# The bonus term of a recurrent attention: from token-major vector work to one d-major product, small matmuls and a seeded PSUM bank

## The chip, the cores and the metric

The kernel runs on one core of one Trainium2 chip, as one program of 961.6 us in the profiled execution. The metric is the device time of the whole program in microseconds, the median of the runs. The engines are named as the profile names them: PE is the matmul engine and PEld its weight loads, DVE the vector engine, ACT the scalar engine, POOL GpSimd, SP the engine that issues most DMAs.

## The reference

The reference chains three parts: a recurrent attention, a capacity-limited mixture of experts on its output, and a second feed-forward network for all tokens. The change touches only the first part:

```python
def _attn_ref(r, k, v, w, u):
    B, H, S, D = r.shape                     # 4, 8, 768, 48
    state = np.zeros((B, H, D, D))
    for t in range(S):
        cur = einsum('bhd,bhe->bhde', u[None] * kt, vt)
        y[:, :, t] = einsum('bhd,bhde->bhe', rt, state + cur)
        state = wt[:, :, :, None] * state + einsum('bhd,bhe->bhde', kt, vt)
```

The term with `cur` is the bonus. Written out, it is for each token and head the number c = sum over d of r·u·k, times the row v of that token: y = r·state + c·v. The 3072 x 384 result y is the input of the routing (logits = y times an 8-column gate) and of the experts (8 experts, 384 tokens each), whose output goes through a network of width 2048.

## The kernel before, in words

The attention is cut into 24 chunks (`NU`) of 128 tokens, six for each of the four batch rows, in the order chunk 0 of all rows, chunk 1 of all rows, and so on. Within a chunk the recurrence is a product of matrices. Two scans along time on DVE (`scans`, L203 and L210) give running products of the decays, Q and Ap. With them, k and r are scaled (`khrh`, L217 on KH, L218 on RH; on POOL except in the first chunks). They are d-major: the 48 features of two heads lie on 112 partitions, the 128 tokens of four head pairs in the free dimension. The steps of a chunk are then:

- `scores` (L265): eight matmuls, KH times RH for each head, into two PSUM tiles `sc`; `scores_ev` (L272): DVE multiplies them with a triangular mask into P.
- `tr` (L253): KH transposed into the bank `pk`; `vp` (L246): v times the gate's weights, also into `pk`. So each head's v carries, behind its 48 columns, 8 columns that make the logits (`vx`, 56 columns a head). ACT copies both out (`vp_ev` L249, `tr_ev` L257).
- `ymm` (L281, L283): state part and score part of y, into the bank `py` (128 x 8 x 56); `umm` (L291): the chunk's addition to the state, into `pu`; `sadd` (L301): DVE adds it to the state `Sb`; `decay` (L306): ACT scales the state.
- the bonus: `rku` (L230, L232) on POOL multiplies token-major r, u and k; `cred` (L237) on DVE sums over the 48 features to c; `cvf` (L242) on POOL makes c times v with its 8 gate columns; `xev` (L313, L320, L316) on DVE adds it to `py`, once for the logits and once for the output `xt`, and reduces the logits over the heads. `xst` stores `xt` to DRAM for the gather of the experts.

The order on each engine is that of the Python code; there is no scheduler that moves it. A loop over n writes, for each n, the PE work of scores(n), tr(n), vp(n), ymm(n-1), umm(n-1), then the DVE work of xev(n-2), scans(n+2), sadd(n-2), scores_ev(n), then ACT's and POOL's. A piece of DVE's other work is threaded in: from n = 8 on parts of a conversion of the last network's weights (`bit`, L850 to L856), from n = 6 on comparisons for the routing (L599), and every fourth n the best expert of four chunks (`top`, L591 to L594). `warm` (L331) issues products of a constant tile into an unused bank before scores(n): 13 ahead of the first chunk, and as `WARMS` says 6, 4 and 2 at n = 1, 3 and 4.

PSUM has few buffers: three for `sc` (two are used per chunk), two for `py`, one each for `pk` and `pu`. So scores(n) needs scores_ev(n-1) for its second tile, and umm(n-1) needs sadd(n-2).

After the attention, from 240 us on, come the routing of the first expert and then eight slots of expert work, which the change does not touch.

Of the kernel before, what the change touches and what calls it, by code (L numbers as in the profile page):

```python
# [9 lines left out]
F32 = mybir.dt.float32  # L10
# [16 lines left out]
E = 8  # L27
# [36 lines left out]
LATE = 4  # L64
# [3 lines left out]
WARMS = {1: 6, 2: 0, 3: 4, 4: 2}  # L68
# [4 lines left out]
class Kernel:  # L73
# [11 lines left out]
    # ------------------------------------------------------------- constants  # L85
# [59 lines left out]
    # ------------------------------------------------- attention, chunk by chunk  # L145
    def attention(self):
        tc, nc, t = self.tc, self.nc, self.t
        with ExitStack() as ctx:
# [9 lines left out]
            ub = A.tile([128, DM], F32, name="ub")  # L158
# [28 lines left out]
            def load2(n):  # L187
                c, b = divmod(n, B)
                d = T[n]
                if n == 0:  # L190
                    nc.sync.dma_start(self.ident, t["cst"][:, 128:256])
                    nc.sync.dma_start(WG, t["wg"])
                nc.sync.dma_start(d["vT"], t["vT"][b, :, c * CH:(c + 1) * CH].rearrange("(a p) t -> p a t", p=128))
                nc.sync.dma_start(d["rkv"], t["rkv"][n])
                if n == 0:
                    nc.sync.dma_start(ub, t["cst"][:, 256:640])
# [29 lines left out]
            def rku(n):  # L226
                d = T[n]
                rk = d["rkv"]
                ku = wk.tile([128, DM], F32, tag="ku", name=f"ku{n}", bufs=2)
                nc.gpsimd.tensor_tensor(ku, rk[:, DM:2 * DM], ub, op=ALU.mult)  # L230
                d["rku"] = wk.tile([128, H, D], F32, tag="rku", name=f"rku{n}", bufs=2)
                nc.gpsimd.tensor_tensor(d["rku"].rearrange("p a b -> p (a b)"), rk[:, 0:DM], ku, op=ALU.mult)  # L232

            def cred(n):
                d = T[n]
                d["cc"] = wk.tile([128, H], F32, tag="cc", name=f"cc{n}")
                nc.vector.tensor_reduce(d["cc"], d["rku"], axis=AX.X, op=ALU.add)  # L237

            def cvf(n):
                d = T[n]  # L240
                d["cv"] = wk.tile([128, H, XW], F32, tag="cv", name=f"cv{n}", bufs=2)
                nc.gpsimd.tensor_tensor(d["cv"], d["vx"], d["cc"].unsqueeze(2).to_broadcast([128, H, XW]), op=ALU.mult)  # L242
# [32 lines left out]
            def ymm(n):  # L275
                d = T[n]
                c, b = divmod(n, B)
                py = d["py"] = ps_y.tile([128, H, XW], F32, tag="py", name=f"py{n}")
                for p in range(NP):
                    if c > 0:  # L280
                        nc.tensor.matmul(py[:, 2 * p:2 * p + 2].rearrange("p a b -> p (a b)"), d["rh"][:R, p], Sb[b][:, p], start=True, stop=False)  # L281
# [3 lines left out]
            def umm(n):  # L285
                d = T[n]
                d["pv"] = ps_u.tile([128, NP, XW], F32, tag="pu", name=f"pu{n}")
# [19 lines left out]

            def xev(n):
                d = T[n]
                d["xt"] = wk.tile([128, H, D], F32, tag="xt", name=f"xt{n}")  # L310
                py = d["py"]
                lg = wk.tile([128, H, E], F32, tag="lg", name=f"lg{n}")
                nc.vector.tensor_tensor(lg, py[:, :, D:], d["cv"][:, :, D:], op=ALU.add)  # L313
                if n < NU - 1:
                    xev2(n)
                nc.vector.tensor_reduce(self.L[:, n], lg.rearrange("p h e -> p e h"), axis=AX.X, op=ALU.add)  # L316

            def xev2(n):
                d = T[n]
                nc.vector.tensor_tensor(d["xt"], d["py"][:, :, :D], d["cv"][:, :, :D], op=ALU.add)  # L320
# [49 lines left out]
            rku(0)  # L370
# [22 lines left out]
            for n in range(NU + 2):  # L393
# [14 lines left out]
                # tensor engine  # L408
                warm(WARMS.get(n, 0))
                if ok(n):  # L410
                    scores(n)
                if ok(n):
                    pk = ps_k.tile([128, 512], F32, tag="pk", name=f"pk{n}")
# [4 lines left out]
                if n == NU - 1:  # L418
                    pb = ps_u.tile([1, 1], F32, tag="pu", name="pb")
                    nc.tensor.matmul(pb, bs[:, 1:2], one, start=True, stop=True)  # L420
                if ok(n - 1):
                    ymm(n - 1)
                if ok(n - 1) and n - 1 < NU - B:
                    umm(n - 1)
                # vector engine
# [3 lines left out]
                if ok(n) and n >= LATE:  # L429
                    cred(n)  # L430
                if n in (2, 3):
                    xev(n - 2)
                    sadd(n - 2)
# [7 lines left out]
                if ok(n - 2) and n > 3:  # L441
                    xev(n - 2)
                next(sg, None)
                if ok(n - 2) and n - 2 < NU - B and n > 3:
                    sadd(n - 2)
                next(sg, None)
# [5 lines left out]
                if n < LATE:  # L452
                    cred(n)
# [9 lines left out]
                if n == NU + 1:  # L463
# [3 lines left out]
                    xev2(NU - 1)  # L467
                # scalar engine
                if ok(n + 1) and n + 1 >= B:
                    decay(n + 1)  # L470
                if ok(n - 2):
                    xst(n - 2)
                if ok(n):
                    vp_ev(n, pk)
                if n < NU - B:
                    tr_ev(n, pk)
# [7 lines left out]
                # gpsimd  # L484
# [3 lines left out]
                if ok(n - 1):  # L488
                    cvf(n - 1)
# [8 lines left out]
                if ok(n + 1):  # L498
                    rku(n + 1)
# [13 lines left out]
    # ------------------ the recurrence step by step, for decays outside [WLO, WHI]  # L513
# [66 lines left out]
    # -------------------------------------------- best expert of each token  # L580
# [33 lines left out]
    def search(self, ph, mk, es, ve):  # L614
        """the expert that fills, and its tokens above the threshold and at it"""
# [47 lines left out]
            # which of them suffice, and the largest  # L663
# [49 lines left out]
    # ------------------ one expert's fill: threshold, tokens, list of token ids.  # L713
    # Yields after each group of vector work and after each group of tensor work.
    def fill(self, ph):
# [4 lines left out]
        if ph == E - 1:  # L720
            # one expert has room: its tokens up to here, and just enough room for all that are left
# [20 lines left out]
        # places in the list, from 1: those above first, then those at it  # L742
# [8 lines left out]
        # place 16 a + b: the ids where b fits, one where a fits, and their product  # L751
# [27 lines left out]
        # place 128 g + j: the ids spread over the partitions j  # L779
# [16 lines left out]
        # what is left for the next one  # L796
# [26 lines left out]
    # ------------------------------------------------------- weights in two parts  # L823
# [19 lines left out]
    def io_bits(self, i):  # L843
        """moe2 weights come as 64-bit floats: their float32 value from the bits"""
# [27 lines left out]
    def io_stages(self):  # L872
        """two pieces at a time, a part of the vector work per step; the other engines follow later"""
# [45 lines left out]
    # ------------------------------------------------------------------ one expert  # L919
# [24 lines left out]
    def slot(self, p, dve, pe, tick):  # L944
# [4 lines left out]
        def product(ps, w):  # L949
            """w: three pairs of parts"""  # L950
# [94 lines left out]
    def rows(self, i):  # L1045
        """the result for the i-th list of tokens: no token is in two lists, so no list waits for another"""
# [122 lines left out]
    def left(self, p):  # L1169
        """the routing after slot p's list and up to the next one"""  # L1170
# [20 lines left out]
def layout(r, k, v, w, u, moe_w_gate, moe_w1, moe_w2, moe2_w_in, moe2_w_out):  # L1191
# [19 lines left out]
    rkv = np.concatenate([token(r).reshape(NU, CH, DM), token(k).reshape(NU, CH, DM), ve.reshape(NU, CH, H * XW)], 2)  # L1211
# [6 lines left out]
    ub = np.broadcast_to(u.reshape(1, DM), (128, DM))  # L1218
# [5 lines left out]
    cst = np.concatenate([mask, np.eye(128, dtype=f), ub], 1)  # L1224
# [21 lines left out]
    a = dict(kr=kr, wp=wp, rkv=rkv, vT=vT, wg=wg, wgp=wgp, uc=uc, cst=cst, kst=kst, w12=w12, wio=wio)  # L1246
# [15 lines left out]
```

## Time and profile before

| | us |
|---|---|
| median of 3 runs | 962.47 (962.35 to 963.18) |
| span of the profiled execution | 961.6 |
| attention, first scores to last y | 8.5 to 240.1 |
| PE busy / DVE busy / ACT busy / POOL busy | 888.7 / 606.9 / 377.6 / 499.8 |

The profile lists one execution. Its span runs from the first to the last instruction, and the timed runs lie about 0.9 us above it. A busy engine is not always a useful one: a DVE instruction's time holds the time for which it was held up while it ran, and a matmul's time depends on the clock that the throttle granted to PE at that moment. That clock has a line of its own on the page, in tenths of the full one.

### The profile page before, as it was taken

How to read it: one execution, taken by the hardware profiler on the slowest of the kernel's cores; microseconds unless marked ns; L12 is line 12 of the kernel's file. 1: busy time of each engine (PE TensorE's matmuls, PEld its weight loads, DVE VectorE, ACT ScalarE, POOL GpSimd, SP SyncE). 2: the span in 40 equal slices, each digit the busy share in tenths (PEclk: the TensorE clock that was granted, in tenths of full speed). 3: DMA queues.
4: the chain of work that ended last, by engine and by line, in shares of the span. 5: the costliest groups of instructions: out<-in, count | busy, mean ns of one | idle time of the engine just before them, and what ended most of it. 6: DMA issues, size and time to landing. Idle time of an engine off the chain costs nothing.

```text
span 961.6 us, 15248 instructions
## 1 busy us (share of the span) xinstructions
PE 888.7 (92%) x5658; PEld 839.9 (87%) x5661; DVE 606.9 (63%) x1333; ACT 377.6 (39%) x865; POOL 499.8 (52%) x441
## 2 busy tenths in 40 slices
PE   7899989999257989999999999999999999999997
PEld 5788978999246979899989999998999999999996
DVE  9999999996789897654466265446635542232211
ACT  3244334330134444344434534443353444334332
POOL 6888756763567356424622732562373365256232
PEclk8675575555567999999999999999999999999999
DMA  9877776620454003102301310220130032023000
GB/s 289 255 223 214 222 212 202 213 82 26 161 189 148 1 0 124 59 1 78 104 1 50 91 42 1 91 91 1 51 107 25 1 107 75 1 75 107 1 1 25
DMA packets 40356, 90.06 MB, mean 94 GB/s; under 512 B 4304, under 2 KB 17104, under 8 KB 40272
## 3 DMA queue, kind: packets, MB, share of 16 engines
q1 hardware_dynamic: 32016, 70.12, 23.7%
q0 software_dynamic: 3072, 9.44, 3.0%
q10 hardware_dynamic: 5184, 9.44, 2.8%
q8 instruction: 46, 0.75, 0.3%
q14 instruction: 38, 0.31, 0.1%
HBM read 79.54 MB, written 9.44 MB: 93 GB/s over the span
## 4 chain that ended last, share of the span: by engine, by line
PE 64%; DVE 28%; issue 3%; DMA 1%; ACT 1%; POOL 1%; POOLq 0%; SPq 0%; ACTq 0%; DVEq 0%
PE pg L953 18%; PE ph L953 8%; PE py L1002 6%; PE py L1004 6%; PE py L1003 6%; PE py L283 3%; DVE cm L647 3%; PE pa L979 3%; PE pa L977 3%; PE pa L978 3%; DVE Ap L210 3%; PE py L281 2%; DVE q L856 2%; DVE Q L203 2%; PE sc L265 2%
## 5 line engine op out<-in xcount | busy, mean ns | idle before, releaser
L994 POOL TENSOR_TENSOR gl<-r,gh 128x384 fp32r<-128x384 f32 x126 | 133.4, 1062 | 268.2 <-ACT gh L993 268.0
L990 DVE SCALAR_TENSOR_TENSOR r<-r,pg 128x384 f32<-128x384 f32 x128 | 70.7, 552 | 158.3 <-ACT r L989 156.4
L953 PE MATMUL pg<-xh,io 128*128 128x384 f32 x768 | 160.8, 344 | 0.0
L906 POOL TENSOR_TENSOR wl<-we,wh 128x768 fp32r<-128x768 f32 x60 | 112.6, 1878 | 59.6 <-ACT wh L905 39.8
L953 PEld LDWEIGHTS pg<-xh,io 128*128 128x128 f32 x768 | 132.2, 188 | 2.6 <-ACT xh L1021 1.6
L1004 PE MATMUL py<-io,gl 128*128 128x384 f32 x384 | 130.4, 340 | 1.7 <-POOL gl L994 1.7
L1002 PE MATMUL py<-io,gh 128*128 128x384 f32 x384 | 131.8, 343 | 0.0
L1003 PE MATMUL py<-io,gh 128*128 128x384 f32 x384 | 129.5, 337 | 0.0
L989 ACT ACTIVATE r<-pg,three 128x384 f32<-128x384 f32 x128 | 74.3, 580 | 118.0 <-PE pg L953 108.3
L993 ACT ACTIVATE gh<-r 128x384 fp32r<-128x384 f32 x128 | 67.2, 525 | 108.6 <-DVE r L990 108.6
L953 PE MATMUL pg<-xl,io 128*128 128x384 f32 x384 | 87.5, 336 | 0.0
L283 PE MATMUL py<-rkv,P 128*128 128x56 f32 x384 | 82.0, 366 | 0.0
L283 PEld LDWEIGHTS py<-rkv,P 128*128 128x128 f32 x384 | 81.5, 298 | 0.0
L971 DVE SCALAR_TENSOR_TENSOR hl<-ph,hh 128x384 fp32r<-128x384 f32 x62 | 34.4, 555 | 68.8 <-ACT hh L970 68.7
L1004 PEld LDWEIGHTS py<-io,gl 128*128 128x128 f32 x384 | 72.4, 189 | 2.7 <-POOL gl L994 2.4
L1002 PEld LDWEIGHTS py<-io,gh 128*128 128x128 f32 x384 | 72.5, 189 | 0.2
L1003 PEld LDWEIGHTS py<-io,gh 128*128 128x128 f32 x384 | 72.6, 189 | 0.0
L905 ACT ACTIVATE wh<-we 128x768 fp32r<-128x768 f32 x64 | 53.6, 838 | 40.6 <-PE pa L979 28.8
L953 PE MATMUL ph<-xh,wh 128*128 128x384 f32 x192 | 68.7, 358 | 0.1
L953 PEld LDWEIGHTS pg<-xl,io 128*128 128x128 f32 x384 | 68.6, 188 | 0.0
L979 PE MATMUL pa<-hl,wh 128*128 128x384 f32 x192 | 65.8, 343 | 0.8 <-POOL hl L968 0.7
L977 PE MATMUL pa<-hh,wh 128*128 128x384 f32 x192 | 66.3, 345 | 0.0
(202 smaller groups left out, 1820.8 us busy)
## 6 DMA issues: line engine op xcount, KB each, us to landing
we<-in_w SPq DMA_DIRECT2D x64, 384.0 KB, 3.1
rkv<-in_rkv SPq DMA_DIRECT2D x24, 608.0 KB, 6.3
kr<-in_kr SPq DMA_DIRECT2D x24, 448.0 KB, 6.4
raw<-in_wio SPq DMA_DIRECT2D x20, 384.0 KB, 6.3
w<-in_wp SPq DMA_DIRECT2D x24, 226.2 KB, 4.4
vT<-in_vT SPq DMA_DIRECT2D x24, 192.0 KB, 4.8
xd<-xt ACTq DMA_DIRECT2D x24, 192.0 KB, 2.9
raw<-in_wio ACTq DMA_DIRECT2D x12, 384.0 KB, 4.4
```

The source lines that it names most:

```text
L283: nc.tensor.matmul(py[:, h], d["P"][h % 2][:, p], d["vx"][:, h], start=(c == 0), stop=(c == 0 or h % 2 == 1))
L906: eng.tensor_tensor(lo, raw, hi, op=ALU.subtract)
L953: nc.tensor.matmul(ps, w[a][part], x[:, a], start=(n == 0), stop=(n == 8))
L977: nc.tensor.matmul(pa[d], wh[:, c], hh, start=(f == 0), stop=False)
L979: nc.tensor.matmul(pa[d], wh[:, c], hl, start=False, stop=(f == NFT - 1))
L989: nc.scalar.activation(g, ph, AF.Relu, bias=self.three)
L990: nc.vector.scalar_tensor_tensor(g, g, 6.0, ph, op0=ALU.min, op1=ALU.mult)
L993: nc.scalar.activation(gh, g, AF.Copy)
L994: (nc.vector if last and f >= NGT - 2 else nc.gpsimd).tensor_tensor(gl, g, gh, op=ALU.subtract)
L1002: nc.tensor.matmul(py[q], gh[:, c], w, start=(f == 0), stop=False)
L1003: nc.tensor.matmul(py[q], gh[:, c], v, start=False, stop=False)
L1004: nc.tensor.matmul(py[q], gl[:, c], w, start=False, stop=(f == NGT - 1))
```

## The change

The bonus is computed another way. `bonus` forms r times k d-major, from the k and r tiles that are loaded anyway, in one DVE multiplication of 112 x 512. `cc` gets c from it with four small matmuls against a constant `UB` that holds u (two columns per pair of heads), into free columns of the bank of `pu`; ACT copies the 8 columns out (`cc_ev`). `seed` writes c times v, with its gate columns, into the bank of `py`: eight ACT instructions of 128 x 56, one per head, with c as the scale. The matmuls of `ymm` then accumulate onto it (start=False everywhere; one product into each of the two `py` buffers at the start of the program sets the state of the bank). So `py` is the finished y: DVE only reduces the logits from it (`logits`), and ACT copies the output (`xev`). POOL loses three multiplications per chunk, DVE three instructions per chunk. The token-major r and k are no longer loaded: 224 KB a chunk for v in place of 608 KB.

The products of the constant tile are now issued in `scores`, into the chunk's own first `sc` tile: 6 for n = 1, none for n = 0 and 2, and 4 for every n from 3 on. Comments were dropped too; they are left out below.

```diff
-LATE = 4
-WARMS = {1: 6, 2: 0, 3: 4, 4: 2}
+WARMS = 0, 6, 0, 4
...
-                d["rkv"] = io.tile([128, 2 * DM + H * XW], F32, tag="rkv", name=f"rkv{n}", bufs=6)
-                d["vx"] = d["rkv"][:, 2 * DM:].rearrange("p (h e) -> p h e", e=XW)
+                d["v"] = io.tile([128, H * XW], F32, tag="v", name=f"v{n}", bufs=6)
+                d["vx"] = d["v"].rearrange("p (h e) -> p h e", e=XW)
...
-            def rku(n):
...
-                nc.gpsimd.tensor_tensor(ku, rk[:, DM:2 * DM], ub, op=ALU.mult)
...
-                nc.gpsimd.tensor_tensor(d["rku"].rearrange("p a b -> p (a b)"), rk[:, 0:DM], ku, op=ALU.mult)
-            def cred(n):
...
-                nc.vector.tensor_reduce(d["cc"], d["rku"], axis=AX.X, op=ALU.add)
-            def cvf(n):
...
-                nc.gpsimd.tensor_tensor(d["cv"], d["vx"], d["cc"].unsqueeze(2).to_broadcast([128, H, XW]), op=ALU.mult)
+            def bonus(n):
+                d["rk"] = wk.tile([R, NP, CH], F32, tag="rk", name=f"rk{n}")
+                nc.vector.tensor_tensor(d["rk"], d["kr"][:, 0], d["kr"][:, 1], op=ALU.mult)
+            def cc(n, pu):
+                d["pc"] = pu[:, 448:448 + H]
+                for p in range(NP):
+                    nc.tensor.matmul(pu[:, 448 + 2 * p:450 + 2 * p], d["rk"][:, p], UB[:, 2 * p:2 * p + 2], start=True, stop=True)
+            def cc_ev(n):
+                nc.scalar.activation(d["cc"], d["pc"], AF.Copy)
+            def seed(n):
+                py = d["py"] = ps_y.tile([128, H, XW], F32, tag="py", name=f"py{n}")
+                for h in range(H):
+                    nc.scalar.activation(py[:, h], d["vx"][:, h], AF.Copy, scale=d["cc"][:, h:h + 1])
...
             def scores(n):
+                for _ in range(WARMS[min(n, len(WARMS) - 1)]):
+                    nc.tensor.matmul(d["sc"][0].rearrange("p a b -> p (a b)"), wz[:, :128], wz, start=True, stop=True)
...
             def ymm(n):
-                py = d["py"] = ps_y.tile([128, H, XW], F32, tag="py", name=f"py{n}")
+                py = d["py"]
...
-                        nc.tensor.matmul(py[:, h], d["P"][h % 2][:, p], d["vx"][:, h], start=(c == 0), stop=(c == 0 or h % 2 == 1))
+                        nc.tensor.matmul(py[:, h], d["P"][h % 2][:, p], d["vx"][:, h], start=False, stop=True, skip_group_check=True)
...
+            def logits(n):
+                nc.vector.tensor_reduce(self.L[:, n], T[n]["py"][:, :, D:].rearrange("p h e -> p e h"), axis=AX.X, op=ALU.add)
             def xev(n):
-                nc.vector.tensor_tensor(lg, py[:, :, D:], d["cv"][:, :, D:], op=ALU.add)
...
-                nc.vector.tensor_reduce(self.L[:, n], lg.rearrange("p h e -> p e h"), axis=AX.X, op=ALU.add)
-                nc.vector.tensor_tensor(d["xt"], d["py"][:, :, :D], d["cv"][:, :, :D], op=ALU.add)
+                nc.scalar.activation(d["xt"], d["py"][:, :, :D], AF.Copy)
...
-            rku(0)
+            for i in range(2):
+                first = ps_y.tile([128, H, XW], F32, tag="py", name=f"first{i}")
+                nc.tensor.matmul(first.rearrange("p a b -> p (a b)"), wz[:, :128], wz[:, :H * XW], start=True, stop=True)
+            bonus(0)
+            bonus(1)
+            pu = ps_u.tile([128, 512], F32, tag="pu", name="pu_")
+            cc(0, pu)
```

PE's order around one chunk, in the kernel before. `pu15` is umm of chunk 15, `cnt8` a sum for the routing, `sc17` the scores of chunk 17, `pk17` its transposes and its gate product:

```order
L291 MATMUL pu15_1757<-rkv15_1122,kt15_1699 48x56 x8
L609 LDWEIGHTS cm8_9_1716
L609 MATMUL cnt8_910<-oh_89,cm8_9_1716 128x8
...
L265 MATMUL sc17_0_1825<-RH2_133,KH2_130 128x128
L265 MATMUL sc17_1_1826<-RH2_133,KH2_130 128x128
...
L253 MATMUL pk17_1835<-ident_72,KH2_130 128x112 x4
L246 MATMUL pk17_1835<-WG_119,vT17_1322 128x64 x3
```

The same place in the changed kernel, after umm of chunk 11; `rk13` is the product r times k of chunk 13, `wz` the constant tile:

```order
L298 MATMUL pu12_1484<-v11_784,kt11_1412 48x56 x8
L234 MATMUL pu12_1484<-UB_118,rk13_1395 128x2 x4
...
L267 LDWEIGHTS wz_136
L267 MATMUL sc13_0_1557<-wz_136 128x512
...
L271 MATMUL sc13_0_1557<-RH1_132,KH1_129 128x128
L271 MATMUL sc13_1_1558<-RH1_132,KH1_129 128x128
...
L257 MATMUL pk13_1571<-ident_72,KH1_129 128x112 x4
L250 MATMUL pk13_1571<-WG_119,vT13_998 128x64 x3
L287 MATMUL py12_1526<-Sb0_123,RH0_131 128x112
```

Four matmuls for c of the next chunk stand behind umm, and four products of the constant tile ahead of the scores; the y of a chunk stands a whole step behind its gate product, as before.

DVE's order in the step n = 13 of the kernel before. `cc13` is cred, Q15 and Ap15 are the scans of chunk 15, `q3` is weight conversion, `lg11`, `xt11` and L belong to xev:

```order
L237 TENSOR_REDUCE cc13_1468<-rku13_1413 128x8
L203 SCALAR_TENSOR_TENSOR Q15_1470<-w15_1119,b1_120 112x517
L206 TENSOR_SCALAR G15_1473<-Q15_1470 112x4
L852 TENSOR_SCALAR q3_1301<-q3_1301 128x384
L313 TENSOR_TENSOR lg11_1477<-py11_1347,cv11_1407 128x64
L320 TENSOR_TENSOR xt11_1476<-py11_1347,cv11_1407 128x384
L316 TENSOR_REDUCE L_87<-lg11_1477 128x8
L208 RECIPROCAL b2_1_122<-G15_1473 112x4
L301 TENSOR_TENSOR Sb3_126<-Sb3_126,pu11_1360 48x4x56 x2
L210 SCALAR_TENSOR_TENSOR Ap15_1471<-w15_1119,b2_1_122 112x517
L272 TENSOR_TENSOR P13_0_1485<-sc13_0_1428,mask_117 128x512
L272 TENSOR_TENSOR P13_1_1487<-sc13_1_1429,mask_117 128x512
```

The same step of the changed kernel; `rk15` is the new multiplication:

```order
L316 TENSOR_REDUCE L_87<-py11_1414 128x8
L201 SCALAR_TENSOR_TENSOR Q15_1607<-w15_1218,b1_120 112x517
L204 TENSOR_SCALAR G15_1610<-Q15_1607 112x4
L858 TENSOR_SCALAR q3_1426<-q3_1426 128x384
L206 RECIPROCAL b2_1_122<-G15_1610 112x4
L308 TENSOR_TENSOR Sb3_126<-Sb3_126,pu12_1484 48x4x56 x2
L228 TENSOR_TENSOR rk15_1616<-kr15_1219 112x512
L208 SCALAR_TENSOR_TENSOR Ap15_1608<-w15_1218,b2_1_122 112x517
L278 TENSOR_TENSOR P13_0_1619<-sc13_0_1557,mask_117 128x512
L278 TENSOR_TENSOR P13_1_1621<-sc13_1_1558,mask_117 128x512
```

The three instructions on `cc`, `lg` and `xt` are gone, the logits' reduction has moved to the head of the step, and one multiplication has come in ahead of the second scan.

PE's first chunk in the kernel before:

```order
L331 MATMUL pw_137<-wz_136 128x512
L265 MATMUL sc0_0_249<-RH0_131,KH0_128 128x128
...
L253 MATMUL pk0_259<-ident_72,KH0_128 128x112 x4
L246 MATMUL pk0_259<-WG_119,vT0_155 128x64 x3
L331 LDWEIGHTS wz_136
```

And in the changed kernel, where `first0` and `first1` are the two products into the `py` buffers:

```order
L373 MATMUL first0_235<-wz_136 128x448
...
L373 MATMUL first1_237<-wz_136 128x448
L234 MATMUL pu__243<-UB_118,rk0_239 128x2 x4
L271 MATMUL sc0_0_258<-RH0_131,KH0_128 128x128
...
L257 MATMUL pk0_268<-ident_72,KH0_128 128x112 x4
L250 MATMUL pk0_268<-WG_119,vT0_155 128x64 x3
L234 MATMUL pu0_290<-UB_118,rk1_241 128x2 x4
```

The first scores now stand behind the four matmuls that read `rk0`, which DVE makes after RH of chunks 0 and 1.

## Rows read from the trace of the kernel before

**Rows 1.** The page, part 2: PE's granted clock in 40 equal slices

```profile
PEclk8675575555567999999999999999999999999999
```

**Rows 2.** Stretches: us, busy us of each engine (instructions), granted clock, DMA

```profile
42.70:76.10 33.40, 29.05 (x262) 27.04 (x261) 32.82 (x56) 13.84 (x42) 27.81 (x31) 0.80 0.79 241
76.10:147.40 71.30, 65.85 (x478) 62.43 (x478) 70.25 (x120) 26.54 (x80) 50.74 (x50) 0.58 0.70 208
147.40:199.00 51.60, 51.60 (x340) 49.28 (x340) 50.91 (x85) 18.74 (x56) 35.60 (x30) 0.50 0.68 215
199.00:240.20 41.20, 41.20 (x248) 39.88 (x246) 32.19 (x71) 7.96 (x24) 19.18 (x17) 0.50 0.07 25
```

**Rows 3.** Timeline of PE, one chunk at half clock: start, us, instruction

```profile
157.68 2.08 PE L265 MATMUL sc<-RH,KH 64*128 64x128 f32 x16
...
160.49 1.41 PE L246 MATMUL pk<-WG,vT 128*128 128x64 f32 x6
161.69 0.71 PE L281 MATMUL py<-Sb,RH 112*128 112x112 f32 x2
...
168.00 2.08 PE L265 MATMUL sc<-RH,KH 64*128 64x128 f32 x16
```

**Rows 4.** Timeline of PE, one chunk at full clock

```profile
134.06 0.60 PE L291 MATMUL pu<-rkv,kt 128*48 128x56 f32 x16
...
134.73 1.54 PE L265 MATMUL sc<-RH,KH 64*128 64x128 f32 x16
136.20 0.60 PE L253 MATMUL pk<-ident,KH 112*128 112x112 f32 x4
136.64 0.79 PE L246 MATMUL pk<-WG,vT 128*128 128x64 f32 x6
137.27 0.43 PE L281 MATMUL py<-Sb,RH 112*128 112x112 f32 x2
...
137.93 0.43 PE L281 MATMUL py<-Sb,RH 112*128 112x112 f32 x2
```

**Rows 5.** Timeline of PE: constant products, scores, and idle time with its cause

```profile
12.21 1.46 PE L331 MATMUL pw<-wz 128*128 128x512 bf16 x6
13.59 1.41 PE L265 MATMUL sc<-RH,KH 64*128 64x128 f32 x16
...
144.40 0.99 PE L291 MATMUL pu<-rkv,kt 128*48 128x56 f32 x16 [4.29 <-DVE Sb L301]
```

**Rows 6.** Groups of DVE, 76.1 to 199 us: instructions, busy us, mean ns

```profile
L599 DVE TENSOR_SCALAR cm<-kst,m 128x256 bf16<-128x256 f32 x12 | 12.0, 1001 | 0.0
...
L320 DVE TENSOR_TENSOR xt<-py,cv 128x384 f32<-128x384 f32 x12 | 6.5, 545 | 0.0
...
L237 DVE TENSOR_REDUCE cc<-rku 128x8 f32<-128x384 f32 x12 | 6.5, 540 | 0.0
```

**Rows 7.** Timeline: the comparison of L599 while POOL is idle

```profile
236.09 0.35 DVE L599 TENSOR_SCALAR cm<-kst,m 128x256 bf16<-128x256 f32 x1
```

**Rows 8.** Groups of DVE, 147 to 240 us: the one RH in it

```profile
L218 DVE TENSOR_TENSOR RH<-kr,Ap 112x512 f32<-112x512 f32 x1 | 0.7, 677 | 0.0
```

**Rows 9.** Groups of POOL, 76.1 to 199 us

```profile
L217 POOL TENSOR_TENSOR KH<-kr,Q 112x512 f32<-112x512 f32 x13 | 26.3, 2025 | 0.0
...
L232 POOL TENSOR_TENSOR rku<-rkv,ku 128x384 f32<-128x384 f32 x12 | 15.2, 1264 | 0.9
L230 POOL TENSOR_TENSOR ku<-rkv,ub 128x384 f32<-128x384 f32 x12 | 14.0, 1164 | 0.0
L242 POOL TENSOR_TENSOR cv<-rkv,cc 128x448 f32<-128x448 f32 x12 | 11.2, 935 | 28.9 <-ACT rkv L249 28.9
```

**Rows 10.** Groups of ACT, 76.1 to 199 us: the decay of the state

```profile
L306 ACT ACTIVATE Sb<-Sb,G 112x112 f32<-112x112 f32 x51 | 15.4, 372 | 0.0
```

**Rows 11.** Timeline of the start: DVE's RH of chunk 1 and first P

```profile
11.94 1.25 DVE L218 TENSOR_TENSOR RH<-kr,Ap 112x512 f32<-112x512 f32 x1
...
13.11 1.27 DVE L272 TENSOR_TENSOR P<-sc,mask 128x512 f32<-128x512 f32 x2
```

More of the change, by code (lines that the diff above doesn't have):

```diff
@@ L157, in attention @@
             mask = A.tile([128, 128], F32, name="mask")
-            ub = A.tile([128, DM], F32, name="ub")
+            UB = A.tile([R, H], F32, name="UB")
             WG = A.tile([128, 3, 64], F32, name="WG")
@@ L224, in check @@
                 nc.scalar.activation(jk, wv, AF.Relu, bias=cb[:, 1:2], scale=1.0, accum_out=acc[:, 2 * n + 1:2 * n + 2])
[L226 removed]
+            def bonus(n):
                 d = T[n]
[L228 to L234 removed]
+                d["rk"] = wk.tile([R, NP, CH], F32, tag="rk", name=f"rk{n}")
+                nc.vector.tensor_tensor(d["rk"], d["kr"][:, 0], d["kr"][:, 1], op=ALU.mult)
+            def cc(n, pu):
+                d = T[n]
+                d["pc"] = pu[:, 448:448 + H]
+                for p in range(NP):
+                    nc.tensor.matmul(pu[:, 448 + 2 * p:450 + 2 * p], d["rk"][:, p], UB[:, 2 * p:2 * p + 2], start=True, stop=True)
+            def cc_ev(n):
                 d = T[n]
                 d["cc"] = wk.tile([128, H], F32, tag="cc", name=f"cc{n}")
[L237 to L239 removed]
+                nc.scalar.activation(d["cc"], d["pc"], AF.Copy)
+            def seed(n):
                 d = T[n]
[L241 to L242 removed]
+                py = d["py"] = ps_y.tile([128, H, XW], F32, tag="py", name=f"py{n}")
+                for h in range(H):
+                    nc.scalar.activation(py[:, h], d["vx"][:, h], AF.Copy, scale=d["cc"][:, h:h + 1])
             def vp(n, pk):
@@ L277, in ymm, with umm @@
                 c, b = divmod(n, B)
-                py = d["py"] = ps_y.tile([128, H, XW], F32, tag="py", name=f"py{n}")
+                py = d["py"]
                 for p in range(NP):
                     if c > 0:
-                        nc.tensor.matmul(py[:, 2 * p:2 * p + 2].rearrange("p a b -> p (a b)"), d["rh"][:R, p], Sb[b][:, p], start=True, stop=False)
+                        nc.tensor.matmul(py[:, 2 * p:2 * p + 2].rearrange("p a b -> p (a b)"), d["rh"][:R, p], Sb[b][:, p],
+                                         start=False, stop=False, skip_group_check=True)
                     for h in (2 * p, 2 * p + 1):
-                        nc.tensor.matmul(py[:, h], d["P"][h % 2][:, p], d["vx"][:, h], start=(c == 0), stop=(c == 0 or h % 2 == 1))
-            def umm(n):
+                        nc.tensor.matmul(py[:, h], d["P"][h % 2][:, p], d["vx"][:, h], start=False, stop=True, skip_group_check=True)
+            def umm(n, pu):
                 d = T[n]
-                d["pv"] = ps_u.tile([128, NP, XW], F32, tag="pu", name=f"pu{n}")
+                d["pv"] = pu[:, 0:NP * XW].rearrange("p (a b) -> p a b", b=XW)
                 for p in range(NP):
@@ L420, in attention @@
                     nc.tensor.matmul(pb, bs[:, 1:2], one, start=True, stop=True)
+                if ok(n):
+                    cc_ev(n)
+                    if n == 0:
+                        vp_ev(0, pk)
+                        tr_ev(0, pk)
+                        seed(0)
                 if ok(n - 1):
                     ymm(n - 1)
-                if ok(n - 1) and n - 1 < NU - B:
-                    umm(n - 1)
+                if ok(n + 1):
+                    pu = ps_u.tile([128, 512], F32, tag="pu", name=f"pu{n}")
+                    if ok(n - 1) and n - 1 < NU - B:
+                        umm(n - 1, pu)
+                    cc(n + 1, pu)
                 bits["room"] = 0 if n < B0 else BITS[n % 4]
@@ L428, in attention @@
                     scores_ev(n)
[L429 to L433, printed above, removed]
+                if ok(n - 2):
+                    logits(n - 2)
                 sg = scans(n + 2) if ok(n + 2) else iter(())
@@ L440, in attention @@
                     flag = nc.values_load(self.bad[0:1, 0:1], min_val=0, max_val=128)
-                if ok(n - 2) and n > 3:
-                    xev(n - 2)
                 next(sg, None)
-                if ok(n - 2) and n - 2 < NU - B and n > 3:
+                if ok(n - 2) and n - 2 < NU - B:
                     sadd(n - 2)
+                if ok(n + 2):
+                    bonus(n + 2)
                 next(sg, None)
@@ L451, in attention @@
                     scores_ev(n)
-                if n < LATE:
-                    cred(n)
                 bit()
@@ L466, in attention @@
                     counted = []
-                    xev2(NU - 1)
+                if ok(n - 2):
+                    xev(n - 2)
+                    xst(n - 2)
                 if ok(n + 1) and n + 1 >= B:
                     decay(n + 1)
-                if ok(n - 2):
-                    xst(n - 2)
-                if ok(n):
+                if ok(n) and n:
                     vp_ev(n, pk)
-                if n < NU - B:
-                    tr_ev(n, pk)
+                    if n < NU - B:
+                        tr_ev(n, pk)
+                    seed(n)
                 if ok(n + 2):
@@ L1217, in layout @@
     wgp = np.ascontiguousarray(moe_w_gate.reshape(3, 128, E).transpose(1, 0, 2))
-    ub = np.broadcast_to(u.reshape(1, DM), (128, DM))
+    ub = np.zeros((R, H), f)
+    ub[0:D, 0::2] = u[0::2].T
+    ub[64:64 + D, 1::2] = u[1::2].T
     uc = np.zeros((R, NP), f)
```

23 lines of the change are left out of this document (5 added, 18 removed).

## The prediction

> **What bounds the kernel now.** I read the table of stretches first, then PE's timeline in two of them, then the groups of DVE and POOL. The page's line of the granted clock [rows 1] shows where to look: from the seventh slice to the fourteenth, inside the attention, PE mostly runs at half clock (1.2 of 2.4 GHz); behind the attention it is at the full one, and the change does nothing there. In the stretches [rows 2] the reader is to see that from 147.4 to 240.2 us PE is busy all the time at a granted 0.50, and that before, from 76.1 on, PE (65.85 of 71.30) and DVE (70.25) are both nearly full. So there is no slack on one engine to hide work of the other. The step of a chunk at half clock, from scores to scores, is 168.00 - 157.68 = 10.32 us [rows 3]. From chunk 8 (76.1) to chunk 20 (199.0) twelve steps take 122.9 us, 10.24 each: PE's length at half clock. At full clock the same work is: addition to the state and the routing's sum 134.73 - 134.06 = 0.67, scores 1.47, transposes 0.44, gate product 0.63, and four groups of y of 0.66 each, 2.64 [rows 4]; in all 5.85 us. DVE would then be the longer one. Before chunk 8 the steps are shorter: four take 33.4 us, 8.35 each, at a mean clock of 0.80 [rows 2], and DVE is the full engine (32.82).
>
> **PE, added.** Four matmuls for c, in fp32 as the gate product is, whose three cost 161.69 - 160.49 = 1.20 us at half clock [rows 3] and 0.63 at full [rows 4]. Their moving side is 2 columns in place of 64, but each has its own weight load of 128 columns as there, so I take the gate product's price: 1.60 at half, 0.84 at full clock. From below it could be a third of that, if the narrow side counted. Four products of the constant tile: six took 13.59 - 12.21 = 1.38 us at full clock [rows 5], so four are 0.92, and about 1.84 at half. The step of PE becomes 5.85 + 0.84 + 0.92 = 7.6 us at full clock and 10.32 + 1.60 + 1.84 = 13.8 at half. Nothing is taken off PE. So the change stands or falls with the clock: the step equals the old 10.24 when (10.24 - 7.6) / (13.8 - 7.6) = 43% of its work runs at half clock.
>
> **PE's clock.** The rows on this: the six products at 12.2 us ran at full clock with the scores behind them (1.41 us instead of 2.08) [rows 5, 3]. Of the steps without such products, from chunk 8 on, most stayed at half clock although PE did not pause (51.60 of 51.60 us) [rows 2]; one rose by itself to 0.67 a group of y [rows 4], and fell back around a wait of 4.29 us for the state's addition on DVE [rows 5]. So a long run of wide products lifts the clock, narrow ones behind weight loads don't, and an idle PE loses it. In the changed kernel each step from chunk 3 on has the wide products and the scores in one piece. I expect a rise in each step at the latest behind the scores, and a fall wherever DVE makes PE wait. If products and scores are paid at half clock and the rest at full, the step is 1.84 + 2.01 + (7.6 - 0.92 - 1.47) = 9.1 us.
>
> The Trainium skill (TensorE: Matmul & The Clock Gate, Why this matters for your kernels) says that matmul throughput is had by keeping TensorE busy without a break. By that rule the stretch at 147 us would already be at full clock and the dummy products would be nothing but cost; the rows, 100% busy at 0.50, are against it.
>
> **DVE.** Off: cred 0.540 and xt 0.545 us [rows 6], and the smaller addition of the logits; the reduction of the logits stays. On: one multiplication 112 x 512 of two SBUF tiles, the size of RH: 0.68 us where POOL left DVE alone [rows 8], 1.25 next to POOL [rows 11]. By itself that is between -0.6 and +0.1 a step. More comes from POOL: the comparison of L599 takes 0.35 us when POOL is idle [rows 7] and 1.00 on the mean of the busy stretch [rows 6], where it runs beside ku and rku. POOL loses ku, rku and cv, 1.16 + 1.26 + 0.94 = 3.4 us a step [rows 9]. That is 0.65 for this instruction, and I take as much again for the scan, the conversion and the little ones that stand in the same shadow; bounds 0 and 2. A DVE step near 10.2 so becomes about 8.6 (9.4 to 7.6).
>
> The Trainium skill (SBUF — State Buffer, Who interferes with whom) has a rule that speaks against the new multiplication: a DVE instruction with two SBUF inputs and a POOL instruction that reads SBUF exclude each other for their whole length, while those removed here read one SBUF input at most. By it `rk` can wait for a KH (2.03 us on the mean [rows 9]) and the step would keep up to 10.6; RH's 1.25 against 0.68 agrees that such a pair holds the other up, but not for a whole KH.
>
> **ACT, POOL, DMA.** ACT gets eight instructions of 128 x 56 with a scale from memory; the decay, 112 wide, takes 0.37 [rows 10], so at most 3.0 a step, plus the output, 0.55 as on DVE, and a copy of 8 columns. It was busy 18.74 of 51.60 us [rows 2], 3.7 a step; it will be busy about 7.5. That hides, since y of a chunk stands a whole step behind its gate product: between them PE has the y, the state's addition and the scores before, at least 5 us, against 0.5 + 3.0 on ACT. Without that cover PE would wait up to 3 us a step. The waits behind a seed on ACT (the check of a later chunk) are early for everyone. DMA moves a quarter less, and was 0.70 busy [rows 2]; at nothing.
>
> **The start.** The matmuls for c of chunk 0 stand ahead of the first scores, and wait for a multiplication that DVE makes behind RH of chunk 1 (ends at 13.19, [rows 11]): first P at about 13.2 + 0.7 + 1.6 + 2.0 = 17.5 us, against 13.11. That is 4.4 us late on an engine that is the full one here. About 3.4 of it should come back by chunk 4, where POOL no longer holds up the scans. +1, bounds -2 and +4.
>
> **The sum**, against the profiled execution (961.6 us; the median is 0.9 above it):
>
> - to 42.7 us: +1
> - four steps to 76.1: 8.35 to 8.0 (PE's clock keeps them from less): -1.4
> - twelve steps to 199: 10.24 to 9.2, between PE's mixed step 9.1 and DVE's 8.6 with their hand-over: -12.5
> - 199 to 240.2, no weight conversion, no state: three steps of 9.65, 8.6 and 8.6 to about 7.5, -4.4; the last scores and two y, 14 us at half clock, to 10.5: -3.5. Together -8
> - after 240.2: 0
>
> -20.9: 940.7 in the span, 942 with what lies around it. With each step from 7.9 to 10.0 the sum runs from 926 to 953.
>
> **Rivals.**
>
> *Full clock and a free DVE.* PE has so little idle time that the clock holds, and POOL's absence is worth 2 us a step. Steps of 8.0: 12 x 2.24 = -27, -3 before, -9 after, +1 at the start: 925. For it: 7.6 fits under DVE's step. Against: then PE waits, and in the trace waits cost the clock.
>
> *The gain is spent.* The rise comes late in each step, or the new multiplication takes up what POOL gave back. The twelve steps stay at 10.2, the end gains 3, the start costs 1: 960.
>
> *Slower: the added PE work is paid at half clock.* The place is the step from chunk 4 on. PE gets 2.4 bound steps more; above 43% of the work at half clock the twelve steps are longer than before. At 60%: 7.6 + 0.6 x 6.2 = 11.3; 12 x 1.1 = +13 and 4 x 2.5 = +10 before (c of the first four chunks has no state part, so it is less than 2.95), +1: 986. All at half clock would be 1030. For it: the trace has 54 us in which full PE work left the clock at 0.50. Against: the rows with constant products.
>
> **How the numbers follow.** Forecast 942: 0.58. Full clock, 925: 0.16. Spent, 960: 0.10, half of it below the bound. Slower, 986: 0.16. A measurement of this kernel tells 0.2%, 1.9 us, from no change. Faster: 0.58 + 0.16 + 0.05 = 0.79; same 0.04; slower 0.17. The likeliest case's own range is 931 to 953. The range that holds 8 in 10 reaches from 922 to 964: it leaves out the slower case but its edge, and the fastest end.
>
> **What would show it.** Right: a granted clock of 0.7 to 0.9 from 76 to 240 us in place of 0.50 to 0.58, scores of 1.4 us behind constant products, steps near 9, L599 well below 1.0 us, ACT near 7.5 us a step without PE waiting for a seed, the first P near 17.5. Wrong: a clock still at 0.5 with PE full and steps above 10.3 (the slower rival), PE idle ahead of y with ACT as its releaser (the cover of the seed gone), or `rk` of 2 us and more beside KH.

## The result, and the profile after

The changed kernel takes 917.92 us (914.75 to 920.66, 4 runs) against 962.41 (962.16 to 963.18, 4 runs): a ratio of 0.954, with a 95% interval of 0.951 to 0.957. The forecast was 942, with a range of 922 to 964; the gain, 44.5 us in place of 20.5, is more than twice the forecast one. Runs over 1.5% above the fastest of their kernel count as slow and stay out of the ratios: below, these are three of the four without products and one of `start`.

The first thing to read is the page's line of the granted clock, which answers to [rows 1]. The long run of fives to sevens there is gone; the dip that is left begins in the ninth slice (183 to 206 us), behind the last y (197 us), in the routing:

```profile
PEclk8899999985879999999999999999999999999998
```

Then the stretches, cut at the same chunks as [rows 2]: scores of chunk 4, 8 and 20, and the last y. The columns are us, busy us of PE, PEld, DVE, ACT and POOL (instructions), granted clock, DMA share, GB/s:

```profile
0.00:43.95 43.95, 34.23 (x266) 27.18 (x269) 37.31 (x62) 24.47 (x74) 13.77 (x22) 0.84 0.92 257
43.95:75.00 31.05, 30.47 (x304) 25.98 (x307) 26.00 (x49) 27.22 (x88) 11.59 (x22) 0.92 0.72 222
75.00:166.80 91.80, 89.51 (x950) 79.04 (x961) 89.05 (x170) 78.16 (x248) 41.62 (x37) 0.99 0.64 194
166.80:197.00 30.20, 28.66 (x270) 25.47 (x273) 25.71 (x62) 22.89 (x73) 8.56 (x7) 1.00 0.09 34
```

| stretch | forecast | measured |
|---|---|---|
| to chunk 4 (before 42.70) | +1 | +1.25 |
| four steps to chunk 8 (33.40) | -1.4 | -2.35 |
| twelve steps to chunk 20 (122.90) | -12.5 | -31.1 |
| to the last y (41.20) | -8 | -11.0 |
| behind it | 0 | -0.7 |
| sum | -20.9 | -43.9 |

So 18.6 of the 23 us that the forecast missed lie in the twelve steps: 7.65 us each, forecast 9.2. PE's timeline shows one of them (start, us, instruction). PE hardly pauses, each piece is at full clock, and from scores to scores it is 112.72 - 105.34 = 7.38 us:

```profile
105.34 1.16 PE L271 MATMUL sc<-RH,KH 64*128 64x128 f32 x16
106.43 0.60 PE L257 MATMUL pk<-ident,KH 112*128 112x112 f32 x4
106.87 0.79 PE L250 MATMUL pk<-WG,vT 128*128 128x64 f32 x6
107.50 0.43 PE L287 MATMUL py<-Sb,RH 112*128 112x112 f32 x2
...
110.27 0.60 PE L298 MATMUL pu<-v,kt 128*48 128x56 f32 x16
110.80 1.05 PE L234 MATMUL pu<-UB,rk 112*128 112x2 f32 x8
111.72 0.19 PE L615 MATMUL cnt<-oh,cm 128*128 128x8 bf16 x2
111.98 0.81 PE L267 MATMUL sc<-wz 128*128 128x512 bf16 x3
112.72 1.16 PE L271 MATMUL sc<-RH,KH 64*128 64x128 f32 x16
```

The matmuls for c take 111.72 - 110.80 = 0.92; the routing's sum and the four products (the profile lists three) 1.00. DVE's busy time is 89.05 us for twelve chunks, 7.42 each, against 10.10 before (70.25 and 50.91 us, [rows 2]). Its groups in that stretch (instructions, busy us, mean ns, idle before):

```profile
L208 DVE TENSOR_TENSOR_SCAN Ap<-w,b 112x517 f32<-112x517 f32 x12 | 18.7, 1554 | 0.0
L201 DVE TENSOR_TENSOR_SCAN Q<-w,b 112x517 f32<-112x517 f32 x11 | 14.7, 1340 | 0.0
L278 DVE TENSOR_TENSOR P<-sc,mask 128x512 f32<-128x512 f32 x22 | 14.2, 685 | 0.3
L228 DVE TENSOR_TENSOR rk<-kr 112x512 f32<-112x512 f32 x12 | 9.1, 756 | 0.4
L605 DVE TENSOR_SCALAR cm<-kst,m 128x256 bf16<-128x256 f32 x11 | 4.7, 429 | 0.0
L204 DVE TENSOR_SCALAR G<-Q 112x4 f32<-112x4 f32 x11 | 3.9, 354 | 0.4
```

The comparison, 1.00 us on the mean before [rows 6], is 0.43, near the 0.35 that it takes beside an idle POOL [rows 7].

### The profile page after: what moved, and what is told of

Its sections match the earlier page's. It is cut to its first block, busy times and chain, and to the rows that moved or that the text cites. A ratio compares the mean times of both kernels' runs of the same rounds, so it can differ in the third digit from the quotient of the medians.

```text
span 917.7 us, 15925 instructions
## 1 busy us (share of the span) xinstructions
PE 849.4 (93%) x5910; PEld 791.7 (86%) x5933; DVE 558.5 (61%) x1285; ACT 448.3 (49%) x1105; POOL 414.2 (45%) x369
## 4 chain that ended last, share of the span: by engine, by line
PE 56%; DVE 16%; issue 2%; ACT 2%; DMA 1%; POOL 1%; POOLq 0%; SPq 0%; ACTq 0%; DVEq 0%
PE pg L959 19%; PE ph L959 9%; PE py L1008 6%; PE py L1010 6%; PE py L1009 6%; DVE cm L653 3%; PE pa L985 3%; PE pa L983 3%; PE pa L984 3%; DVE q L862 2%; DVE q L860 1%; DVE q L856 1%; DVE r L996 1%; PE cnt L663 1%; DVE q L858 1%
## 5 line engine op out<-in xcount | busy, mean ns | idle before, releaser
L976 ACT ACTIVATE hh<-ph 128x384 fp32r<-128x384 f32 x62 | 30.4, 491 | 77.8 <-PE ph L959 77.8
L959 PE MATMUL ph<-xh,wl 128*128 128x384 f32 x192 | 65.8, 342 | 0.0
```

Source lines behind the costliest of these rows:

```text
L959: nc.tensor.matmul(ps, w[a][part], x[:, a], start=(n == 0), stop=(n == 8))
```

## The experiments

Two theories stood after the result. F: the constant products hold PE's clock. W: the clock is full because DVE, with POOL out of its way, no longer makes PE wait. The first runs take the parts one at a time.

**No products.**

```diff
-WARMS = 0, 6, 0, 4
+WARMS = 0, 6, 0, 0
```

> The changed kernel without the four constant products of each chunk from n = 3 on (n = 1 keeps its six); nothing else differs. Theory F (the constant products hold the clock): without them the clock falls to half in most of the steps from 76 us on; PE's step at half clock is 10.3 plus 1.8 for c, about 12, so the time rises to 950 to 1005 us and the granted clock from 75 us to the end of the attention is 0.5 to 0.75. Theory W (the clock is full because DVE, with POOL out of its way, no longer lets PE wait): the clock stays above 0.95 there, and the step falls from 7.4 to DVE's own 7.2, so 910 to 917 us.

Measured: 953.05 us in the profiled execution; the other three took 982.07, 982.25 and 990.75, the median is 982.16. In the profile the clock is at half for 37.5 us, at full for 54.6 and at half again for 61.5. These stretches, and PE's timeline at the second fall:

```profile
35.30:72.80 37.50, 37.50 (x235) 35.59 (x234) 25.19 (x49) 23.09 (x73) 8.78 (x16) 0.50 0.58 169
72.80:127.40 54.60, 53.48 (x603) 50.53 (x603) 48.28 (x104) 49.25 (x159) 21.25 (x27) 1.00 0.74 214
127.40:188.90 61.50, 61.50 (x390) 59.19 (x388) 48.22 (x85) 38.20 (x118) 25.45 (x17) 0.50 0.42 127
```

```profile
125.97 1.16 PE L271 MATMUL sc<-RH,KH 64*128 64x128 f32 x14 [0.25 <-DVE P L278]
127.06 0.70 PE L257 MATMUL pk<-ident,KH 112*128 112x112 f32 x4
127.55 1.40 PE L250 MATMUL pk<-WG,vT 128*128 128x64 f32 x6
...
134.91 1.87 PE L234 MATMUL pu<-UB,rk 112*128 112x2 f32 x8
136.64 0.20 PE L615 MATMUL cnt<-oh,cm 128*128 128x8 bf16 x2
136.76 2.08 PE L271 MATMUL sc<-RH,KH 64*128 64x128 f32 x16
```

In both stretches at half clock PE is busy all the time (37.50 and 61.50 us); the step there is 148.79 - 136.76 = 12.03 us (expected 12). So both theories hold a piece: once at full the clock lasts without products while PE hardly waits (W), but once lost it takes long to come back (F). It does come back, at 72.8 and at 188.9 us, so the products are not needed for a rise. The fall stands 1.4 us behind a wait of 0.25 us for DVE's mask. Waits of 0.15, 0.24 and 0.48 us in the three steps before passed without one, so that the wait caused it is not shown.

**The products alone**, in the kernel before:

```diff
             def scores(n):
+                for _ in range((0, 6, 0, 4)[min(n, 3)]):
+                    nc.tensor.matmul(d["sc"][0].rearrange("p a b -> p (a b)"), wz[:, :128], wz, start=True, stop=True)
...
-                warm(WARMS.get(n, 0))
```

> The kernel before with the constant products alone: 6 at n = 1, none at n = 0 and 2, 4 for every n from 3 on, in the chunk's own scores tile, as in the changed kernel; the bonus stays as it was. Theory F: the clock rises to 0.9 or more from 76 us on, but DVE is full at 10.1 us a step, so only the last stretch (199 to 240 us, where PE alone was full) becomes shorter, by 6 to 10 us: 950 to 958 us. Theory W: DVE makes PE wait, the clock stays between 0.5 and 0.7 and the added products are paid at half clock: 970 us or more.

Measured: 959.57 us (955.48 to 963.86), ratio 0.996 (0.992 to 1.000). The clock rises, 0.82 against 0.56 in the same stretch of the kernel before, and buys next to nothing, because DVE is full:

```profile
75.00:167.00 92.00, 74.67 (x640) 61.93 (x648) 90.71 (x153) 34.40 (x103) 63.67 (x60) 0.82 0.73 216
```

F's time, slightly missed on the slow side, and a clock between the theories. The products alone give 0.4%, not clear of no change. The new bonus alone gave 1.1% in its fastest run (953.05 against 963.46; a single run) and was 2 to 3% slower than the kernel before in the other three. Both together give 4.6%, more than the sum of the parts: the gain is an interaction.

**POOL's work put back** into the changed kernel, with outputs that nobody reads:

```diff
+            def load_a(n):
+                f = T[n]["kr"].rearrange("p a b c -> p (a b c)")
+                for i in range(2):
+                    x = wk.tile([R, DM], F32, tag=f"x{i}", name=f"x{i}_{n}", bufs=2)
+                    nc.gpsimd.tensor_tensor(x, f[:, 0:DM], f[:, 512:512 + DM], op=ALU.mult)
+            def load_b(n):
+                x = wk.tile([128, H * XW], F32, tag="x2", name=f"x2_{n}", bufs=2)
+                nc.gpsimd.tensor_tensor(x, T[n]["v"], T[n]["v"], op=ALU.mult)
```

> The changed kernel with three multiplications a chunk put back on POOL (two of 112 x 384, one of 128 x 448, outputs unused), where ku, rku and cv stood. If POOL's work held DVE's instructions up by about 2 us a step, the DVE step goes from 7.4 to about 9.4 and the time rises by 20 steps of 2, 30 to 45 us, to 947 to 963, with PE idle part of each step; whether the clock then falls tells theory W from F: F keeps it above 0.9 (step 9.4), W lets it fall below 0.75 (step 10 or more). If the DVE step is shorter only because of the instructions taken off it, the time stays at 917 to 922.

Measured: 966.68 us (964.78 to 970.39). That is 48.8 us more, so the whole gain is gone. It lies 4 us beyond the range expected, with the clock at 0.81 from 75 to 167 us. That left open how much is DVE held up and how much the clock, so it was run again with eight products (`WARMS = 0, 6, 0, 8`):

> The changed kernel with POOL's three multiplications back (as in 'pool_load') and eight constant products a chunk from n = 3 on, so that the clock has no reason to fall: PE's step at full clock is 7.37 + 4 x 0.21 = 8.2 us, below the DVE step of 9.2 to 9.8 that 'pool_load' showed from 82 to 100 us. If the 49 us of 'pool_load' are DVE held up by POOL, the clock is above 0.95, PE idles 1 us a step, and the time is 950 to 965. If half of them came from the clock, it is 935 to 948.

Measured: 959.13 us (958.04 to 960.15, 10 runs). The clock is back at 0.94 (expected above 0.95) and DVE is full from scores of chunk 8 to those of chunk 20, 117.54 of 119.27 us:

```profile
82.04:201.31 119.27, 107.16 (x1010) 86.92 (x1009) 117.54 (x179) 81.15 (x256) 84.69 (x76) 0.94 0.50 151
```

That is twelve chunks of 9.94 us with DVE busy for 9.80, against 7.65 and 7.42: the same DVE instructions take 2.4 us a chunk more beside a busy POOL. So 41 of the 49 us remain with the clock nearly full, 27 of them in these twelve chunks, and go with DVE held up; about 7.5 go with the clock. DVE's groups from 75 to 200 us show where:

```profile
L208 DVE TENSOR_TENSOR_SCAN Ap<-w,b 112x517 f32<-112x517 f32 x13 | 25.7, 1974 | 0.0
L201 DVE TENSOR_TENSOR_SCAN Q<-w,b 112x517 f32<-112x517 f32 x13 | 20.3, 1561 | 0.0
L289 DVE TENSOR_TENSOR P<-sc,mask 128x512 f32<-128x512 f32 x24 | 15.5, 687 | 0.4
L228 DVE TENSOR_TENSOR rk<-kr 112x512 f32<-112x512 f32 x13 | 14.5, 1117 | 0.4
L620 DVE TENSOR_SCALAR cm<-kst,m 128x256 bf16<-128x256 f32 x12 | 8.9, 745 | 0.0
L204 DVE TENSOR_SCALAR G<-Q 112x4 f32<-112x4 f32 x13 | 8.5, 650 | 0.4
```

Ap +0.42, Q +0.22, `rk` +0.36, the comparison and G +0.3 each; P, which reads PSUM, is unchanged at 0.69.

**How many products.** Two and six in place of four:

> The changed kernel with two constant products a chunk from n = 3 on, in place of four. Theory F (they bring the clock back after a fall, and hold it): with half as many the clock falls more often and stays low longer, some of 982 us (none) and 918 (four): 930 to 965 us, a granted clock of 0.8 to 0.95 from 75 us to the end of the attention. Rival D (they only have to be there; four are too many): the clock holds as with four and the step falls by 2 x 0.21 to DVE's 7.2 us: 912 to 917 us.

Measured: 928.01 us (919.05 to 931.19), clock 0.93 from 75 to 167 us. Rival D is out; F's range was 2 us too high.

> The changed kernel with six constant products a chunk from n = 3 on. At full clock each costs PE 0.21 us, so a step is 7.8 in place of 7.37 us where PE is the bound. Theory F with four being just enough: no fall from chunk 4 on saves the two that the profile of the changed kernel shows (about 4 us) and 21 x 0.43 = 9 us are added: 919 to 925 us, runs within 2 us of each other. If four leave the clock low for longer in many executions, six are faster: 908 to 917.

Measured: 919.80 us (919.46 to 921.74); the step is 7.81, the clock 1.00 from 44 to 197 us. Six cost PE what they save; the spread falls from 5.9 us to 2.3. The count weighs a price paid in every step against falls in some.

**No bonus at all**: the kernel before with the four products, POOL's and DVE's bonus instructions taken out, the bonus left out of y:

```diff
-                    cred(n)
-                    cvf(n - 1)
-                    rku(n + 1)
-                nc.vector.tensor_tensor(lg, py[:, :, D:], d["cv"][:, :, D:], op=ALU.add)
-                nc.vector.tensor_tensor(d["xt"], d["py"][:, :, :D], d["cv"][:, :, :D], op=ALU.add)
+                nc.scalar.activation(d["xt"], d["py"][:, :, :D], AF.Copy)
```

> The kernel before with the four constant products and without the bonus: no rku, cred, cvf on POOL and DVE, no addition of the bonus to the logits and the output (ACT copies the output); its term is left out of y. Nothing of the new form (rk, c, seed) is in it. Theory F with POOL's shadow of 2 us: DVE's step is 7.4 - 0.76 = 6.7 us and PE's 6.5 at full clock, the clock holds above 0.9, and the time is 895 to 915 us: the gain of the change comes from what is taken off POOL and DVE, and the new form costs 0 to 20 us of it. Rival N (the products of c and the seed are needed to keep PE busy enough): the clock falls below 0.8 because PE waits, and the time is 930 us or more.

Measured: 896.72 us (896.00 to 906.09), clock 1.00. PE's step is 90.02 - 83.53 = 6.49 us:

```profile
83.53 1.16 PE L267 MATMUL sc<-RH,KH 64*128 64x128 f32 x16
...
89.06 1.02 PE L263 MATMUL sc<-wz 128*128 128x512 bf16 x4
90.02 1.16 PE L267 MATMUL sc<-RH,KH 64*128 64x128 f32 x16
```

Rival N is out: c's products are not needed for the clock. The token-major r and k are still loaded here (264 GB/s from 75 to 167 us, against 194 in the changed kernel), so the lighter load is not needed for a short DVE step either. The step is 0.89 shorter than the changed kernel's: of the new form only the four matmuls for c (0.92) show in it. Scores of chunk 23 stand at 165.35 in place of 189.31; 5.8 of these 24 us are there at chunk 4 (38.14 for 43.95), where the start without c counts too, and 18.2 come from the 19 steps behind it. So the bonus still costs some 21 us, of which c's matmuls are some 17 (19 of 0.92).

**The start.** c of chunk 0 behind its scores:

```diff
-            bonus(0)
-            bonus(1)
-            pu = ps_u.tile([128, 512], F32, tag="pu", name="pu_")
-            cc(0, pu)
...
                     vp(n, pk)
+                if n == 0:
+                    scores_ev(0)
+                    bonus(0)
+                    pu = ps_u.tile([128, 512], F32, tag="pu", name="pu_")
+                    cc(0, pu)
+                    bonus(1)
```

> The changed kernel with another order at chunk 0: the multiplication r k and the four matmuls for c of chunk 0 stand behind its scores, transposes and mask, not ahead of them. If the late first scores cost what the first stretch lost, scores of chunk 0 start at about 9 us in place of 15.2, its first P at about 13, and chunk 4 one to four us earlier: 913 to 916 us. If the start is bounded by the loads (DMA 0.92 busy there), chunk 4 starts at the same 44 us and the time stays at 917 to 919.

Measured: 923.28 us (915.66 to 932.23), not the 913 to 916 expected. The start itself does what was expected: first scores at 8.68, chunk 4 at 41.60 in place of 43.95, chunk 17 at 136.65 in place of 142.22. Then, in the profiled execution, PE waits for a mask at 162 us, the clock falls, and the next two scores stand 14 and 12 us apart in spite of the products (PE's timeline):

```profile
162.25 1.96 PE L271 MATMUL sc<-RH,KH 64*128 64x128 f32 x14 [0.54 <-DVE P L278]
...
173.79 1.49 PE L267 MATMUL sc<-wz 128*128 128x512 bf16 x3 [0.24 <-issue]
175.21 2.08 PE L271 MATMUL sc<-RH,KH 64*128 64x128 f32 x16
...
187.20 2.08 PE L271 MATMUL sc<-RH,KH 64*128 64x128 f32 x16
```

The changed kernel has such a wait too (0.53 at 167.81 us) and kept its clock there. So six products from chunk 17 on were tried with the new start, `WARMS = (0, 6, 0) + 14 * (4,) + (6,)`:

> The order of chunk 0 as in the run 'start' (c of chunk 0 behind its scores), and six constant products from n = 17 on, where every second chunk of 'start' made PE wait 0.5 to 0.7 us for DVE's mask and the clock fell at 163 us for two chunks. If the fall behind that wait is what spent the better start (chunk 17 stood 5.6 us earlier there than in the changed kernel), the time is 908 to 916 us, below the changed kernel. If the earlier start itself brings the falls, it stays at 918 to 926.

Measured: 915.09 us (914.45 to 917.27), the lowest median of the kernels with the bonus, ratio 0.952 (0.950 to 0.954). The fall at 163 us is gone; its profile has a shorter one at 145 us. And with six in chunks 3 to 8 as well, beside the changed kernel itself:

> The order of 'start', with six constant products for chunks 3 to 8 and from 17 on, four between (chunks 9 to 16, where the clock held in every profile with four and POOL light). If falls in the early and the late chunks are what is left to gain, they are gone: 912 to 915 us, narrower than the 3 us of 'start_late6'. If four were enough early, the six early chunks cost 6 x 0.43 = 2.6 us: 916 to 918.

> The changed kernel itself, for its spread beside the other two on one chip. Its clock falls at different chunks in different executions if the falls hang on where in the step they are looked for: runs from 914 to 921 us, median 916 to 919.

Measured: 917.86 us (916.77 to 918.74) and 918.29 (916.25 to 920.57). Six early show no gain: the ratio of `start_both6` is 0.954 (0.952 to 0.957). The intervals of `start_late6` and of the changed kernel overlap too; its gain of 3 us is possible, not shown.

## Why the prediction was wrong

*The bound and the kind of gain* were read rightly: PE at half clock, no slack, a change that stands or falls with the clock, nothing behind 240 us. What happened is the mechanism of the rival "full clock and a free DVE", to which I gave 0.16 and 925 us.

*The step that failed first* is "a fall wherever DVE makes PE wait" and, from it, the mixed step of 9.1 us with products and scores paid at half clock in each. In the stretch of twelve steps one began at half clock; the rest ran at full, at 7.38 us where PE did not wait. Falls and waits for DVE do not go together in the profile of the changed kernel. From chunk 0 to the last y the clock falls three times. Two falls, at 49.5 and 73.4 us, stand behind stretches in which PE was busy all the time:

```profile
44.00:49.40 5.40, 5.40 (x67) 5.15 (x67) 4.50 (x8) 4.79 (x17) 1.82 (x7) 1.00 0.92 287
49.40:52.90 3.50, 3.26 (x21) 2.11 (x21) 2.25 (x6) 3.02 (x10) 1.18 (x1) 0.51 0.85 261
66.65:73.30 6.65, 6.65 (x78) 6.37 (x79) 5.69 (x10) 6.01 (x21) 2.71 (x5) 1.00 0.75 239
73.30:76.80 3.50, 3.32 (x21) 2.16 (x21) 3.21 (x8) 3.05 (x11) 2.19 (x2) 0.51 1.02 305
```

The third fall, at 32.4 us, stands behind a wait of 1.10 us for a seed on ACT. Waits of 0.65, 0.53 and 0.64 us for DVE's mask, in chunks 18, 20 and 22, passed at full clock; the first of them:

```profile
152.04 1.16 PE L271 MATMUL sc<-RH,KH 64*128 64x128 f32 x14 [0.65 <-DVE P L278]
```

Where PE waits for more of its time, as with the products alone (74.67 us busy of 92.00), the clock is lower all the same, 0.82.

I read the 54 us at half clock in the trace as a state into which PE drops back; the run without products shows that the full clock lasts just as well, 54.6 us, while PE hardly waits. It also shows the clock rise with narrow matmuls alone (72.8 and 188.9 us), against what I took from the rows. With the products the clock was back sooner: the three stretches at half clock here last 3.4 to 6.8 us, though one in `start` lasted 27.

*The second* is DVE's step: forecast 8.6, measured 7.42. POOL's shadow was taken as 1.3 us, with bounds of 0 and 2. The step fell by 10.10 - 7.42 = 2.68 us; the instructions taken off (0.54, 0.55 and 0.21) and put on (0.76) make 0.54 of it, so 2.1 are left for the shadow. The run with POOL's work put back gives 2.4, with `rk`'s 0.36 among them. I had one instruction with both durations, L599, and doubled it; L599 gave 0.57, and the scans, conversions and clamps in the same shadow 1.6 in place of 0.65. The two failed steps belong together. With DVE at 8.6, PE at 7.6 would have waited a microsecond in every step. At 7.42 against 7.38 it waits for 2.3 of 91.8 us.

The Trainium skill (SBUF — State Buffer, Who interferes with whom) would have named the rows: under conditions on their operands it counts copies and tensor_scalar forms among the DVE instructions that can contend with POOL, beside those with two SBUF inputs. The trace agrees: the scans and `rk` (two SBUF inputs), the comparison and G (tensor_scalar) are longer beside POOL's added work (Ap 1.97 against 1.55 us), P, with one input in PSUM, is not (0.69 and 0.69). I used the rule only against `rk`.

*PE's terms.* 7.6 was forecast at full clock, 7.38 measured. The scores were taken at 1.47 from a row [rows 4] that was at full clock throughout, but in which DVE still worked on the mask of the chunk before (two P, 134.37 to 135.66 us) that the second `sc` tile needs; with P done they are 1.09. c is 0.92 (forecast 0.84), at half clock 136.64 - 134.91 = 1.73 (1.60).

*The last stretch*: its three steps take 22.52 us against 26.89, -4.4 as forecast; the last scores and two y 7.7 us against a forecast 10.5, at full clock throughout.

*`rk` and ACT.* `rk` is 0.756 on the mean of the twelve steps, within 0.68 and 1.25, and at most 0.81, so it does not wait for a KH there. ACT is busy 78.16 us for twelve chunks, 6.5 each (forecast 7.5), its seeds 0.31 each. Up to 200 us PE waits for a seed twice, once in the start and once here:

```profile
31.98 0.65 PE L298 MATMUL pu<-v,kt 128*48 128x56 f32 x16 [1.10 <-ACT py L246]
148.46 0.60 PE L298 MATMUL pu<-v,kt 128*48 128x56 f32 x16 [0.69 <-ACT py L246]
```

*The start* came as forecast: the first P at 17.28 (forecast 17.5), behind PE's longest wait for DVE, and +1.25 us at chunk 4:

```profile
13.37 1.87 PE L234 MATMUL pu__243<-UB,rk 112*128 112x2 f32 x8 [6.77 <-DVE rk L228]
15.17 2.08 PE L271 MATMUL sc<-RH,KH 64*128 64x128 f32 x16
```

*Open*: what makes the clock fall. It fell with PE busy all the time, and held over waits of 0.65 us; no experiment here sets when it falls, and so the 6 us by which the runs of the changed kernel spread are not explained either.

## What to carry to other kernels

An edit can be worth nothing alone and much beside another: products that lift the clock give 0.4% while another engine is the bound, and taking work off that engine gave at most 1.1% while the clock is mostly low. Where two engines are nearly full, work out the step of each with both changes made, and ask which waits then, before taking a mean between clock states. Work on POOL is priced by what it does to DVE's instructions beside it: collect every DVE group whose mean differs with POOL busy and idle, not one of them.

## What the runs showed of the hardware

- The same work ran for long at either clock: without wide products PE's fp32 matmuls kept 1.00 from 72.8 to 127.4 us, and were at 0.50 for 37.5 us before and 61.5 us behind, busy all the time.
- A 112 x 4 clamp (G) takes 0.17 us in the median, but 0.65 on the mean beside the busiest POOL (`pool_load_8`) and once 1.92; its size doesn't bound what it loses there.
- Matmuls with two columns on the moving side cost 0.92 us for four in fp32, more than the gate product's three with 64 columns (107.50 - 106.87 = 0.63): 0.21 to 0.23 each, with 2 columns as with 64.
